# Global-query scores as eight 64x32 products over two key halves, with maxima exchanged on GpSimd

## The chip, the cores and the metric

The kernel runs on one core of one Trainium2 chip. A core has a matrix engine (TensorE; PE in the rows, with PEld for its weight loads), a vector engine (VectorE, DVE), a scalar engine (ScalarE, ACT), GpSimd (POOL), a queue engine (SyncE, SP) and 16 DMA engines. SBUF is the working memory of 128 partitions, PSUM the memory of 8 banks into which TensorE writes. The metric is the device time of one execution in microseconds (us); lower is better.

## What is computed

Two stages, all in float32. First attention, with batch 8, 8 heads, 512 local and 32 global tokens of width 64. Each global query looks at all 544 keys; each local query looks at the 32 global keys and at the local keys within 32 positions. Then a soft mixture of experts over the 4352 resulting rows.

```
k_all = np.concatenate([k_g, k_l], axis=2)
s_g   = scale * np.matmul(q_g, k_all.transpose(0, 1, 3, 2))
out_g = np.matmul(sm(s_g), v_all)                  # sm: exp(s - max) / (sum + 1e-9)
s_l   = scale * [q_l @ k_g.T, where(|i - j| <= 32, q_l @ k_l.T, -1e9)]
out_l = np.matmul(sm(s_l), np.concatenate([v_g, v_l], axis=2))
x     = rows of concatenate([out_g, out_l], axis=2)
logits = x @ phi                                   # then softmax over tokens and over slots,
slot_out[e] = relu(slot_input[e] @ w1[e]) @ w2[e]  # experts, and c @ slot_out
```

The change concerns `s_g` and `sm(s_g)` alone.

## The kernel before

Attention runs in 32 steps. Step s handles two heads: the upper 64 partitions of the tile `kq` hold the transposed keys and queries of one head, the lower 64 those of the other. Every engine runs its instructions in the order in which the program issues them; `step(s)` writes that order by hand. In step s TensorE does, in this order: scores of step s+1 into the PSUM tile `pS` (`scores`; it begins with the mask products that read `cb`), turns of the shifted scores of step s into `pT` (`turn_pair`, operands `con,w`), turns of finished rows (`con,x`) and of shifted global scores (`con,sgs`) into `pM`, value products of step s-1 into `pO` (`values`, first with 32 columns, last with 64), and between those, in odd steps, the value products of global queries (`v,eg`) and the logits (`xT,phisb`, when s % 4 = 1) or the token sums (`x,dd`, when s % 4 = 3).

Global queries are handled for two steps, that is four heads, at once: i = s // 2 runs from 0 to 15. Four heads of 32 queries fill 128 partitions.

- `global_scores(i)` (line 309) stands last on TensorE in the even step 2i. The query operand has 64 columns, 32 for each of two heads, and zeros in the other head's partitions, so that a product over all 128 partitions gives both heads. Per `kq` tile there is a product of 480 key columns into bank 0 of `pM` and one of 64 into bank 1. ScalarE copies both into `sgr` (608 columns).
- `global_max(i)` (line 321) reduces `sgr` on VectorE to `gm` in the odd step; `global_shift(i)` (line 325) subtracts the maximum on ScalarE, `sgr` to `sgs`, near the end of the odd step, behind `og`.
- `turn_global` turns `sgs` on TensorE in the next two steps, `exp_global` takes the exponential on ScalarE into `eg`, and `global_values` multiplies by the values.

At the end of an odd step VectorE normalises the step's rows (`x`, line 303) and computes `rg` (line 365) for the global queries before; ScalarE scales them (`og`, line 371), shifts (`sgs`, line 326) and, when s % 4 = 1, copies the logits out of `pM` (`lT`, line 544). When s % 4 = 3 VectorE adds the token sums (`acc`, line 449). The next step's turns on TensorE write the banks that `lT` and `acc` read, and read `sgs`.

GpSimd makes two shifted copies of the values per step (`make_v`, `va` and `vb`) and, in odd steps, four copies of `og` into `xg`.

Loads of `kq`, `v` and of expert weights `w` are issued by `pump` whenever the count `npe` of TensorE instructions passes a multiple of 256 after `PHASE`; the load then waits for that TensorE instruction. A float32 product counts as four instructions: two passes, each with a weight load. After the steps come the experts, which the change leaves as they were.

Of the kernel before, what the change touches and what calls it, by code (L numbers as in the profile page):

```python
# [17 lines left out]
P = 128  # L18
VD = D + 1
NP = 4 * B  # L20
NEG = -8.0e9
GUARD = 1e-9
SCALE = 0.125

ROW0, ROW1, QONE, ROW2, GCOPY, SQ = 0, 6, 11, 12, 17, 23
SQG = SQ + 15
NSLOT = SQG + 2  # L30
KQC = 32 * NSLOT


BANKS = [[0, 13, 11, 12], [1, 4, 7, 10], [2, 5, 8, 14], [3, 6, 9, 15]]
PAIRED = ((0, 0), (2, 3))
IN_ROW = [(q, i) for i in range(4) for q in range(4) if (q, i) != (3, 1)]
Q_SLOT = {(3, 1): QONE, **{qi: SQ + k for k, qi in enumerate(IN_ROW)}}
BLK_POS = {c: (k, i) for k, cs in enumerate(BANKS) for i, c in enumerate(cs)}
TOK = {4: 0, 7: 1}
LW = P + NS  # L40
GW = 608
VG = (0, 1, 2, 3, 5)

C_ID, C_Q, C_EM, C_ONE = 0, 128, 256, 258
# [22 lines left out]
def kernel(ctx, tc, kq, vS, phi, w1, w2, cst, cbf, out):  # L67
    nc = tc.nc
# [16 lines left out]
    pM = psum.tile([P, 2, 512], F32, name="pM")  # L85
# [13 lines left out]
    dT = keep.tile([P, LW], F32, name="dT")  # L99
    dd = keep.tile([P, P], F32, name="dd")  # L100
    de = keep.tile([P, NS], F32, name="de")
    sgr = at.tile([P, GW], F32, name="sgr")
    sgs = at.tile([P, GW], F32, name="sgs")
    eg = at.tile([P, 5, P], F32, name="eg")

    def bc(ap, n):
# [17 lines left out]
    def mm(o, l, r, start=True, stop=True):  # L124
        return counted(2 if l.dtype == BF16 else 4, nc.tensor.matmul(o, l, r, start=start, stop=stop))  # L125
# [180 lines left out]


    def global_scores(i):
        for pp in range(2):
            k = kqs[2 * i + pp]  # L310
            q = k[:, SQG:SQG + 2, :]
            mm(pM0[HALF[pp], 0:480], q, at_cols(k, FULL, 0, [(192, 3), (32, 5), (1, 32)]))
            mm(pM1[HALF[pp], 0:64], q, at_cols(k, FULL, 32 * 5, [(32 * (GCOPY - 5), 2), (1, 32)]))
        nc.scalar.copy(at_cols(sgr, FULL, 0, [(32, 3), (P, 5), (1, 32)]),
                       pM0[:, 0:480].rearrange("p (r m j) -> p r m j", r=3, m=5))
        nc.scalar.copy(at_cols(sgr, FULL, 480, [(-384, 2), (1, 32)]),
                       pM1[:, 0:64].rearrange("p (a j) -> p a j", a=2))

    gm = {}

    def global_max(i):
        gm[i] = xp.tile([P, 1], F32, tag="gm", name=f"gm{i}")
        nc.vector.tensor_reduce(gm[i], sgr, axis=AX.X, op=ALU.max, negate=True)

    def global_shift(i):
        nc.scalar.activation(sgs, sgr, AF.Identity, bias=gm[i])  # L326


    def turned(c, n, w=P, t=pM):
        return t[0:w, :, c:c + 64 * n].rearrange("p r (u q) -> p u r q", q=64)  # L330

# [10 lines left out]

    def turn_global(n, c0=CG, t=pM):
        units = []
        for u, m in enumerate((0, 1, 2) if n == 0 else (3, 5)):
            lo, w = (P * m, 96 if m == 3 else P) if m < 4 else (480, P)
            units.append(turn_to(c0 + 64 * u, sgs[:, lo:lo + w], w, t))
        return both(units)

    def exp_global(n, c0=CG, t=pM):  # L350
        for m, u, k, w in (((0, 0, 3, P),) if n == 0 else ((3, 0, 1, 96), (4, 1, 1, P))):
            nc.scalar.activation(split(eg[0:w, m:m + k, :]), turned(c0 + 64 * u, k, w, t), AF.Exp, scale=SCALE)  # L352

    def global_values(i, bank):
        for n, m in enumerate(VG):
            for j in range(4):
                mm(bank[32 * j:32 * j + 32, 0:VD], eg[:, n, 32 * j:32 * j + 32],
                   vs[2 * i + j // 2][:, m, j % 2, :], n == 0, n == 4)

    rgs = {}  # L360
# [99 lines left out]
    for _ in range(4):  # L460
        issue(queue)
    nc.sync.dma_start(phisb, phi)
    nc.gpsimd.memset(sgr, NEG)
    nc.gpsimd.memset(eg, 0.0)
    nc.vector.memset(guard, GUARD)
    nc.scalar.activation(lrun, guard, AF.Exp)
    npe[0] = 48
# [5 lines left out]
    def step(s):  # L473
# [64 lines left out]
        if q == 2 and s >= 6:  # L538
            totals(b - 1)
        if not ev:  # L540
            global_shift(i)
        if q == 1 and b >= 1:
            w = LW if b - 1 in TOK else P
# [17 lines left out]
    exp_global(0)  # L561
    nc.scalar.copy(split(dd.unsqueeze(1)), turned(CD, 1))
    copy_tokens(s - 2, nc.vector.tensor_copy)
    global_shift(i)
    values(s - 1, (1,))
    global_values(i - 1, gO)
# [284 lines left out]
def _layout(inputs):  # L851
# [8 lines left out]

    rows = [list(range(0, 16, 3)), list(range(1, 16, 3)), list(range(2, 16, 3))]
    both = np.concatenate([chunks(k_l, k_g), chunks(q_l, q_g)], axis=2)
    seq = rows[0] + rows[1] + [17 + BANKS[3][1]] + rows[2] + [16] * 6 + [17 + BANKS[q][i] for q, i in IN_ROW] + [33, 33]
    kq = both[:, :, seq].reshape(B, 4, 2, KQC, D).transpose(0, 1, 2, 4, 3).reshape(NP, P, NSLOT, 32)
    kq = np.ascontiguousarray(kq)
    kq[:, 64:, SQG] = 0
    kq[:, :64, SQG + 1] = 0
    vc = np.ones((B, H, 17, 32, VD), q_l.dtype)
    vc[..., :D] = chunks(v_l, v_g)
    vseq = sum([[3 * m, 3 * m + 1, 3 * m + 2, 16] for m in range(5)], []) + [15, 12, 13, 14]  # L870
# [48 lines left out]
```

## Time and profile before

| | us |
|---|---|
| timed runs | 264.94, 266.04, 268.48 (median 266.04) |
| the profiled execution | 264.19 |
| its span, first to last instruction | 262.4 |
| TensorE busy | 228.8 (87%) |
| VectorE busy | 161.2 (61%) |
| ScalarE busy | 118.7 (45%) |
| GpSimd busy | 100.9 (38%) |

Busy time is an average over the attention steps (about 10 to 195 us) and the experts behind them. The chain of waits follows the work that ended last back from the end; "issue" in it is time in which an engine waited for nothing that the profile shows. A matmul's time in a row includes the time in the array's pipeline, so that consecutive products overlap in the rows; how long a stage holds TensorE is read from the start of its first row to the start of the next stage.

### The profile page before, as it was taken

The numbers are of one execution on the slowest core, as the hardware profiler recorded it, in microseconds if no ns is written. First come the engines' busy times: TensorE is split into PE (matmuls) and PEld (weight loads), VectorE is DVE, ScalarE is ACT, GpSimd is POOL, SyncE is SP. The second block draws the span as 40 slices with busy tenths as digits, with TensorE's granted clock in tenths as the row PEclk, the third lists the DMA queues.
The fourth block names the chain that finished last, engine by engine and source line by source line (L and its number), as shares of the span: only waits on it lengthen the run. The fifth ranks groups of instructions, "written<-read, shape, count | busy, mean of one in ns | idle before, by whom it ended". The sixth has DMA issues, their size and how long they took to land.

```text
span 262.4 us, 14172 instructions
## 1 busy us (share of the span) xinstructions
PE 228.8 (87%) x6435; PEld 157.8 (60%) x6435; DVE 161.2 (61%) x281; ACT 118.7 (45%) x292; POOL 100.9 (38%) x196
## 2 busy tenths in 40 slices
PE   8789988998998998899799988969879999999910
PEld 5477666686766757576675865757655344545700
DVE  0777756876777775767577868745634673144810
ACT  2235727556555653656545555715832031132810
POOL 2484537384482835547380845534510000000000
PEclk9999999999999999999999999997999999999975
DMA  7958968779879687776868687798999999985997
GB/s 237 374 206 254 331 237 257 249 289 299 288 252 318 210 275 229 276 257 235 333 188 313 217 302 273 241 374 336 303 382 361 417 406 410 408 317 198 370 352 256
DMA packets 26636, 77.61 MB, mean 296 GB/s; under 512 B 2384, under 2 KB 8784, under 8 KB 26576
## 3 DMA queue, kind: packets, MB, share of 16 engines
q1 hardware_dynamic: 22400, 65.12, 70.7%
q10 hardware_dynamic: 4176, 11.58, 12.1%
q8 instruction: 50, 0.82, 1.2%
q14 instruction: 10, 0.08, 0.1%
HBM read 67.78 MB, written 8.91 MB: 292 GB/s over the span
## 4 chain that ended last, share of the span: by engine, by line
PE 73%; DVE 10%; issue 7%; ACT 5%; ACTq 0%; DVEq 0%
PE pO L125 16%; PE pS L125 12%; PE pM L125 11%; PE pM L128 6%; PE kT L125 5%; PE kM L125 5%; PE pT L128 4%; PE kS L125 4%; PE kO L125 4%; DVE x L303 3%; PE pM L456 2%; DVE mx L249 2%; DVE w L251 1%; ACT sgs L326 1%; DVE acc L449 1%
## 5 line engine op out<-in xcount | busy, mean ns | idle before, releaser
L249 DVE TENSOR_REDUCE mx<-pS 128x8 f32<-128x1024 f32 x31 | 37.7, 1217 | 16.5 <-PE pS L125 16.5
L125 PE MATMUL pS<-kq 64*64 64x128 f32 (+1 forms) x1736 | 41.2, 279 | 3.8 <-issue 3.8
L375 POOL COPY xg<-og 32x64 f32<-32x64 f32 x62 | 14.3, 231 | 75.1 <-ACT og L371 73.2
L125 PE MATMUL pO<-v,w 128*32 128x65 f32 x620 | 40.6, 224 | 1.0 <-issue 0.9
L125 PE MATMUL pO<-va,w 128*32 128x65 f32 x620 | 40.9, 226 | 0.0
L251 DVE TENSOR_TENSOR w<-pS,mx 128x1024 f32<-128x1024 f32 x31 | 38.0, 1225 | 1.1
L125 PEld LDWEIGHTS pS<-kq 64*64 64x64 f32 (+1 forms) x1736 | 30.8, 111 | 12.6 <-issue 10.2
L125 PEld LDWEIGHTS pO<-v,w 128*32 128x32 f32 x620 | 32.1, 115 | 8.2 <-issue 6.5
L258 ACT ACTIVATE w<-pT 128x1024 f32<-128x1024 f32 x32 | 32.5, 1017 | 9.2 <-PE pT L128 9.2
L125 PEld LDWEIGHTS pO<-va,w 128*32 128x32 f32 x620 | 31.9, 115 | 3.0 <-issue 1.0
L352 ACT ACTIVATE eg<-pM 96x128 f32<-96x128 f32 (+2 forms) x45 | 13.9, 343 | 33.3 <-PE pM L128 32.6
L267 POOL COPY va<-v 128x650 f32<-128x650 f32 x32 | 23.2, 725 | 13.0 <-DMA v<-in_vS_dram 11.7
L125 PE MATMUL pO<-vb,w 128*32 128x65 f32 x496 | 27.6, 221 | 0.4 <-issue 0.4
L292 ACT ACTIVATE r<-pO,guard 128x8 f32<-128x8 f32 x31 | 8.3, 267 | 39.1 <-PE pO L125 39.0
L128 PE MATMUL pT<-con,w 64*128 64x64 f32 x512 | 23.1, 230 | 1.6 <-DVE w L251 0.8
L268 POOL COPY va<-v 32x650 f32<-32x650 f32 x32 | 23.1, 722 | 2.0
L128 PEld LDWEIGHTS pT<-con,w 64*128 64x128 f32 x512 | 18.6, 139 | 8.2 <-issue 2.9
L303 DVE TENSOR_TENSOR x<-pO,r 128x512 f32<-128x512 f32 x31 | 21.4, 692 | 3.2
L125 PEld LDWEIGHTS pO<-vb,w 128*32 128x32 f32 x496 | 22.2, 109 | 0.6 <-issue 0.6
L295 DVE RECIPROCAL r<-r 128x8 f32<-128x8 f32 x32 | 6.5, 202 | 23.5 <-ACT r L292 23.3
L269 POOL COPY vb<-v 64x520 f32<-64x520 f32 x32 | 19.8, 620 | 1.9
L270 POOL COPY vb<-v 64x520 f32<-64x520 f32 x32 | 19.7, 614 | 1.7
(204 smaller groups left out, 429.7 us busy)
## 6 DMA issues: line engine op xcount, KB each, us to landing
w<-in_w_dram SPq DMA_DIRECT2D x60, 512.0 KB, 6.3
kq<-in_kq_dram SPq DMA_DIRECT2D x32, 640.0 KB, 4.9
v<-in_vS_dram ACTq DMA_DIRECT2D x29, 390.0 KB, 5.1
out_dram<-ob SPq DMA_DIRECT2D x16, 512.0 KB, 4.6
xw<-in_w_dram SPq DMA_DIRECT2D x4, 512.0 KB, 7.0
v<-in_vS_dram SPq DMA_DIRECT2D x3, 390.0 KB, 6.9
out_dram<-ob SPq DMA_DIRECT2D x2, 256.0 KB, 4.8
cb<-in_cbf_dram SPq DMA_DIRECT2D x1, 272.0 KB, 2.9
```

The lines of the kernel that those rows point to most:

```text
L125: return counted(2 if l.dtype == BF16 else 4, nc.tensor.matmul(o, l, r, start=start, stop=stop))
L128: return counted(2, nc.tensor.transpose(o, src, idn))
L249: nc.vector.reduce_max(mx, g, axis=AX.X)
L251: nc.vector.tensor_tensor(ws[s], g, bc(mx, P), ALU.subtract)
L258: nc.scalar.activation(ws[s], pT.rearrange("p r (u q) -> p (r u q)", q=64), AF.Exp, scale=SCALE)
L267: nc.gpsimd.tensor_copy(va, v[:, 0:5])
L268: nc.gpsimd.tensor_copy(va[0:32], v[0:32, 1:6])
L269: nc.gpsimd.tensor_copy(vb[64:128], v[64:128, 0:4])
L270: nc.gpsimd.tensor_copy(vb[0:64], v[0:64, 1:5])
L303: nc.vector.tensor_tensor(xs[b][:, :, P * p:P * p + P].rearrange("p t (h d) -> p h t d", h=2), o[:, :, :, 0:D], bc(r.rearrange("p (h t) -> ...
L352: nc.scalar.activation(split(eg[0:w, m:m + k, :]), turned(c0 + 64 * u, k, w, t), AF.Exp, scale=SCALE)
L375: copy(xgs[b // 4][32 * (b % 4):32 * (b % 4) + 32, D * hd:D * hd + D], og[32 * j:32 * j + 32, :])
```

## The change

The query operand has 32 columns and no zeros. Each head's product runs over its own 64 partitions, and the 576 key columns (the 17 chunks of 32 keys, with the global chunk twice) are taken in two halves of 288: half x goes into bank x of `pM`. For a `kq` tile pp, a partition half hh and a key half x the output goes to partitions 32c to 32c+31 with c = 2pp + (hh xor x): in the second half neighbouring heads have changed places. So eight products of 64 partitions, 32 output partitions and 288 columns stand in place of four, on eight different parts of the array. One ScalarE copy of 576 columns brings them to `sgr`.

Each half has its own maximum (`gx`, two columns), and since the halves of a head lie on different partitions, GpSimd copies `gx` to `gy` with neighbouring groups of 32 partitions exchanged (four copies of 32x2); `global_both` on VectorE combines the two into `gm`, one column for each half. The shift becomes three ScalarE instructions of 288, 192 and 64 columns with a bias from `gm`; `sgs`, now 640 columns wide, is filled once with NEG where `eg` was cleared before. The second exponential becomes one instruction where there were two, and all turns have 128 columns. The value products of the second half read `eg` with the heads changed back. The size of `kq` stays the same: a second zero-padded query slot is given up, and `QONE` moves into the row of queries.

```
-ROW0, ROW1, QONE, ROW2, GCOPY, SQ = 0, 6, 11, 12, 17, 23
-SQG = SQ + 15
-NSLOT = SQG + 2
+ROW0, ROW1, GONE, ROW2, GCOPY, SQ = 0, 6, 11, 12, 17, 23
+SQG = SQ + 16
+NSLOT = SQG + 1
...
     def global_scores(i):
-        for pp in range(2):
-            k = kqs[2 * i + pp]
-            q = k[:, SQG:SQG + 2, :]
-            mm(pM0[HALF[pp], 0:480], q, at_cols(k, FULL, 0, [(192, 3), (32, 5), (1, 32)]))
-            mm(pM1[HALF[pp], 0:64], q, at_cols(k, FULL, 32 * 5, [(32 * (GCOPY - 5), 2), (1, 32)]))
-        nc.scalar.copy(at_cols(sgr, FULL, 0, [(32, 3), (P, 5), (1, 32)]),
-                       pM0[:, 0:480].rearrange("p (r m j) -> p r m j", r=3, m=5))
-        nc.scalar.copy(at_cols(sgr, FULL, 480, [(-384, 2), (1, 32)]),
-                       pM1[:, 0:64].rearrange("p (a j) -> p a j", a=2))
+        for x in range(2):
+            for hh in range(2):
+                for pp in range(2):
+                    k, c = kqs[2 * i + pp], 2 * pp + (hh ^ x)
+                    mm(pM[32 * c:32 * c + 32, x, 0:GH], k[HALF[hh], SQG, :],
+                       at_cols(k, HALF[hh], 96 * x, [(192, 3), (32, 3), (1, 32)]))
+        nc.scalar.copy(sgr, pM[:, :, 0:GH])
...
     def global_max(i):
-        gm[i] = xp.tile([P, 1], F32, tag="gm", name=f"gm{i}")
-        nc.vector.tensor_reduce(gm[i], sgr, axis=AX.X, op=ALU.max, negate=True)
+        gx[i] = [xp.tile([P, 2], F32, tag=n, name=f"{n}{i}") for n in ("gx", "gy")]
+        nc.vector.tensor_reduce(gx[i][0], sgr, axis=AX.X, op=ALU.max, negate=True)
+        for c in range(4):
+            R, O = (slice(32 * k, 32 * k + 32) for k in (c, c ^ 1))
+            nc.gpsimd.tensor_copy(gx[i][1][R], gx[i][0][O])
+
+    def global_both(i):
+        gm[i] = xp.tile([P, 2], F32, tag="gm", name=f"gm{i}")
+        x, y = gx.pop(i)
+        nc.vector.tensor_tensor(gm[i], x, at_cols(y, FULL, 1, [(-1, 2)]), ALU.min)
...
     def global_shift(i):
-        nc.scalar.activation(sgs, sgr, AF.Identity, bias=gm[i])
+        for c, d, dst, src in ((0, 0, [(32, 3), (P, 3), (1, 32)], [(96, 3), (32, 3), (1, 32)]),
+                               (3 * P, GH, [(32, 3), (160, 2), (1, 32)], [(96, 3), (32, 2), (1, 32)]),
+                               (4 * P, GH + 64, [(-32, 2), (1, 32)], [(192, 2), (1, 32)])):
+            nc.scalar.activation(at_cols(sgs, FULL, c, dst),
+                                 bass.AP(sgr.tensor, sgr.offset + d, [list(sgr.ap[0])] + [list(e) for e in src]),
+                                 AF.Identity, bias=gm[i][:, (c > 0):(c > 0) + 1])
...
     def exp_global(n, c0=CG, t=pM):
-        for m, u, k, w in (((0, 0, 3, P),) if n == 0 else ((3, 0, 1, 96), (4, 1, 1, P))):
-            nc.scalar.activation(split(eg[0:w, m:m + k, :]), turned(c0 + 64 * u, k, w, t), AF.Exp, scale=SCALE)
+        k = 3 - n
+        nc.scalar.activation(split(eg[:, 3 * n:3 * n + k, :]), turned(c0, k, P, t), AF.Exp, scale=SCALE)
...
         if not ev:
+            global_both(i)
             global_shift(i)
```

On TensorE, at the end of an even step, the order before (a row of a product stands for its two passes; `kq_294` and `kq_387` are the tiles of the two steps):

```order
L125 MATMUL pO<-v_296,w_381 64x65
L125 MATMUL pO<-va_458,w_381 64x65
L125 MATMUL pM<-kq_294 64x480
L125 MATMUL pM<-kq_294 64x64
L125 MATMUL pM<-kq_387 64x480
L125 MATMUL pM<-kq_387 64x64
L125 LDWEIGHTS cb
```

and now (the same place; `kq_282` and `kq_388` are the same two tiles):

```order
L126 MATMUL pO<-v_284,w_396 64x65
L126 MATMUL pO<-va_471,w_396 64x65
L126 MATMUL pO<-v_284,w_396 64x65
L126 MATMUL pO<-va_471,w_396 64x65
L126 MATMUL pM<-kq_282 32x288
L126 MATMUL pM<-kq_388 32x288
```

The last two rows come four times in turn, and then the mask products (`cb`) follow as before: eight products with 32 output partitions where four with 64 stood.

On ScalarE, at the end of an odd step with s % 4 = 1 and the start of the next, before:

```order
L258 ACTIVATE w_646<-pT 128x1024
L371 ACTIVATE og_881<-pO,rg_878 128x64
L326 ACTIVATE sgs<-sgr,gm_765 128x608
L544 COPY lT<-pM 128x128
L352 ACTIVATE eg<-pM 96x128
L352 ACTIVATE eg<-pM 128x128
L385 COPY xT_965<-pM 128x512
```

and now:

```order
L259 ACTIVATE w_668<-pT 128x1024
L385 ACTIVATE og_910<-pO,rg_907 128x64
L338 ACTIVATE sgs<-sgr,gm_916 128x3x3x32
L338 ACTIVATE sgs<-sgr,gm_916 128x3x2x32
L338 ACTIVATE sgs<-sgr,gm_916 128x2x32
L558 COPY lT<-pM 128x128
L365 ACTIVATE eg<-pM 128x256
L399 COPY xT_997<-pM 128x512
```

Three shifts stand between `og` and `lT` where one stood; behind the turns one exponential stands for two.

On VectorE, from the reduction of `sgr` in an odd step with s % 4 = 3 to the next step, now (before, the fourth last row was not there, and the first wrote `gm`, one column):

```order
L324 TENSOR_REDUCE gx_1089<-sgr 128x2
L296 RECIPROCAL r_1192<-r_1192 128x8
L304 TENSOR_TENSOR x_905<-pO,r_1192 128x2x4x64
L378 TENSOR_SCALAR rg_1197<-pO 128x1
L379 RECIPROCAL rg_1197<-rg_1197 128x1
L332 TENSOR_TENSOR gm_1206<-gx_1089,gy_1090 128x2
L461 COPY acc<-pM 128x512
L250 TENSOR_REDUCE mx_1250<-pS 128x8
L252 TENSOR_TENSOR w_1252<-pS,mx_1250 128x1024
```

The combining step stands behind four other instructions after the reduction; between the two, GpSimd has its four copies `gy`, ahead of `xg`.

## Rows read from the trace of the kernel before

**Rows 1.** The page: busy us and instructions, a queue (packets, MB), the chain.
```profile
PE 228.8 (87%) x6435; PEld 157.8 (60%) x6435; DVE 161.2 (61%) x281; ACT 118.7 (45%) x292; POOL 100.9 (38%) x196
...
q8 instruction: 50, 0.82, 1.2%
...
PE 73%; DVE 10%; issue 7%; ACT 5%; ACTq 0%; DVEq 0%
```

**Rows 2.** Attention: busy PE, PEld, DVE, ACT, POOL (instructions); clock, DMA share, GB/s.
```profile
10.00:195.00 185.00, 165.27 (x5652) 124.24 (x5652) 130.37 (x204) 99.83 (x244) 99.02 (x190) 0.99 0.81 276
```

**Rows 3.** Waits of TensorE, 10 to 195 us: total us, times, longest.
```profile
PE pS L125 <- issue: 5.5, 4, 1.7
...
PE pM L125 <- issue: 3.6, 3, 2.4
...
PE pO L125 <- issue: 2.6, 5, 0.9
...
PE pS L125 <- DVE w L251: 1.3, 2, 0.7
```

**Rows 4.** TensorE by time, end of an even step: start, us, what.
```profile
97.55 0.22 PE L125 MATMUL pO<-va,w 128*64 128x65 f32 x1
...
98.67 0.41 PE L125 MATMUL pS<-cb 64*64 64x512 bf16 x4
```

**Rows 5.** TensorE by time, end of an odd step.
```profile
93.26 0.22 PE L125 MATMUL pO<-va,w 128*64 128x65 f32 x1
93.41 0.41 PE L125 MATMUL pS<-cb 64*64 64x512 bf16 x4
```

**Rows 6.** TensorE by time, four 32x32 products into one bank, experts' start.
```profile
200.03 0.63 PE L125 MATMUL kM<-xg,de 32*32 32x256 f32 x8
200.60 0.42 PE L125 MATMUL kM<-x,dd 128*32 128x256 f32 x4
```

**Rows 7.** ScalarE by time, end of an odd step with logits.
```profile
83.79 0.31 ACT L371 ACTIVATE og<-pO,rg 128x64 f32<-128x64 f32 x1 [0.48 <-DVE rg L365]
84.00 0.79 ACT L326 ACTIVATE sgs<-sgr,gm 128x608 f32<-128x608 f32 x1
84.70 0.25 ACT L544 COPY lT<-pM 128x128 f32<-128x128 f32 x1
```

**Rows 8.** TensorE by time behind it.
```profile
85.00 0.46 PE L128 MATMUL pM<-con,x 64*128 64x64 f32 x8 [0.85 <-ACT lT L544]
```

**Rows 9.** ScalarE and TensorE by time, ends of two odd steps with token sums.
```profile
51.33 0.79 ACT L326 ACTIVATE sgs<-sgr,gm 128x608 f32<-128x608 f32 x1
...
52.18 0.32 PE L128 MATMUL pM<-con,sgs 64*96 64x64 f32 x4
...
166.34 0.79 ACT L326 ACTIVATE sgs<-sgr,gm 128x608 f32<-128x608 f32 x1
...
167.19 0.32 PE L128 MATMUL pM<-con,sgs 64*96 64x64 f32 x4
```

**Rows 10.** GpSimd by time in an odd step; a two-operand VectorE instruction, min/median/max ns.
```profile
84.17 1.05 POOL L375 COPY xg<-og 32x64 f32<-32x64 f32 x4 [4.43 <-ACT og L371]
...
L415 DVE TENSOR_TENSOR nm<-bm,nm x7: 159/160/1124, 65.2 to 197.7; 128x1 f32<-128x1 f32 x7
```

**Rows 11.** The last step by time: GpSimd, ScalarE, TensorE.
```profile
186.48 0.62 POOL L270 COPY vb<-v 64x520 f32<-64x520 f32 x1
...
187.22 0.80 ACT L326 ACTIVATE sgs<-sgr,gm 128x608 f32<-128x608 f32 x1 [0.57 <-DVE gm L323]
...
192.03 0.77 PE L125 MATMUL pS<-v,eg 128*32 128x65 f32 x39 [1.72 <-issue]
```

**Rows 12.** The chain in time: its longest pause.
```profile
174.17 2.37 issue
```

**Rows 13.** The stretch behind that pause, columns as in rows 2.
```profile
177.50:181.00 3.50, 3.50 (x77) 2.44 (x78) 1.32 (x5) 2.24 (x5) 0.60 (x3) 0.51 0.89 343
```

More of the change, by code (lines that the diff above doesn't have):

```diff
@@ L35 @@
 PAIRED = ((0, 0), (2, 3))
-IN_ROW = [(q, i) for i in range(4) for q in range(4) if (q, i) != (3, 1)]
-Q_SLOT = {(3, 1): QONE, **{qi: SQ + k for k, qi in enumerate(IN_ROW)}}
+IN_ROW = [(q, i) for i in range(4) for q in range(4)]
+Q_SLOT = {qi: SQ + k for k, qi in enumerate(IN_ROW)}
 BLK_POS = {c: (k, i) for k, cs in enumerate(BANKS) for i, c in enumerate(cs)}
@@ L40 @@
 LW = P + NS
-GW = 608
+GH = 288
 VG = (0, 1, 2, 3, 5)
@@ L101 @@
     de = keep.tile([P, NS], F32, name="de")
-    sgr = at.tile([P, GW], F32, name="sgr")
-    sgs = at.tile([P, GW], F32, name="sgs")
+    sgr = at.tile([P, 2, GH], F32, name="sgr")
+    sgs = at.tile([P, 5 * P], F32, name="sgs")
     eg = at.tile([P, 5, P], F32, name="eg")
@@ L319 @@
-    gm = {}
-    def global_max(i):
-        gm[i] = xp.tile([P, 1], F32, tag="gm", name=f"gm{i}")
-        nc.vector.tensor_reduce(gm[i], sgr, axis=AX.X, op=ALU.max, negate=True)
-    def global_shift(i):
-        nc.scalar.activation(sgs, sgr, AF.Identity, bias=gm[i])
+        for x in range(2):
[4 more added lines that the diff above has]
+                       at_cols(k, HALF[hh], 96 * x, [(192, 3), (32, 3), (1, 32)]))
@@ new lines, in global_scores @@
+        nc.scalar.copy(sgr, pM[:, :, 0:GH])
+    gm, gx = {}, {}
+    def global_max(i):
+        gx[i] = [xp.tile([P, 2], F32, tag=n, name=f"{n}{i}") for n in ("gx", "gy")]
[7 more added lines that the diff above has]
+        nc.vector.tensor_tensor(gm[i], x, at_cols(y, FULL, 1, [(-1, 2)]), ALU.min)
@@ L344, in turn_global @@
         units = []
-        for u, m in enumerate((0, 1, 2) if n == 0 else (3, 5)):
-            lo, w = (P * m, 96 if m == 3 else P) if m < 4 else (480, P)
-            units.append(turn_to(c0 + 64 * u, sgs[:, lo:lo + w], w, t))
+        for u, m in enumerate((0, 1, 2) if n == 0 else (3, 4)):
+            units.append(turn_to(c0 + 64 * u, sgs[:, P * m:P * m + P], P, t))
         return both(units)
     def exp_global(n, c0=CG, t=pM):
-        for m, u, k, w in (((0, 0, 3, P),) if n == 0 else ((3, 0, 1, 96), (4, 1, 1, P))):
-            nc.scalar.activation(split(eg[0:w, m:m + k, :]), turned(c0 + 64 * u, k, w, t), AF.Exp, scale=SCALE)
+        k = 3 - n
+        nc.scalar.activation(split(eg[:, 3 * n:3 * n + k, :]), turned(c0, k, P, t), AF.Exp, scale=SCALE)
     def global_values(i, bank):
@@ L356, in global_values @@
             for j in range(4):
-                mm(bank[32 * j:32 * j + 32, 0:VD], eg[:, n, 32 * j:32 * j + 32],
+                c = j if n < 3 else j ^ 1
+                mm(bank[32 * j:32 * j + 32, 0:VD], eg[:, n, 32 * c:32 * c + 32],
                    vs[2 * i + j // 2][:, m, j % 2, :], n == 0, n == 4)
@@ L462 @@
     nc.sync.dma_start(phisb, phi)
-    nc.gpsimd.memset(sgr, NEG)
-    nc.gpsimd.memset(eg, 0.0)
+    nc.gpsimd.memset(sgs, NEG)
     nc.vector.memset(guard, GUARD)
@@ L563 @@
     copy_tokens(s - 2, nc.vector.tensor_copy)
+    global_both(i)
     global_shift(i)
@@ L862, in _layout @@
     both = np.concatenate([chunks(k_l, k_g), chunks(q_l, q_g)], axis=2)
-    seq = rows[0] + rows[1] + [17 + BANKS[3][1]] + rows[2] + [16] * 6 + [17 + BANKS[q][i] for q, i in IN_ROW] + [33, 33]
+    seq = rows[0] + rows[1] + [16] + rows[2] + [16] * 6 + [17 + BANKS[q][i] for q, i in IN_ROW] + [33]
     kq = both[:, :, seq].reshape(B, 4, 2, KQC, D).transpose(0, 1, 2, 4, 3).reshape(NP, P, NSLOT, 32)
     kq = np.ascontiguousarray(kq)
-    kq[:, 64:, SQG] = 0
-    kq[:, :64, SQG + 1] = 0
     vc = np.ones((B, H, 17, 32, VD), q_l.dtype)
```

## The prediction, made before the result was known

> **What bounds the kernel now.** I read the shares of the chain first, to see which engine ends last: TensorE holds 73% of it and VectorE 10% [rows 1]. So the reader should look for time that leaves or enters TensorE's stream. Attention is next, from 10 to 195 us: TensorE is busy there for 165.27 of 185 us [rows 2]. Then the waits of TensorE in that stretch: the largest is "issue", 5.5 + 3.6 + 2.6 = 11.7 us in twelve pauses [rows 3], in which nothing that the profile shows held it. What is it? The page has 50 packets, 0.82 MB in all, on the instruction queue, 16 KB each, and TensorE and its loads have 2 x 6435 = 12870 instructions [rows 1], some 257 for a packet. Counted through the trace, these pauses lie 256 instructions or a multiple of it apart. I conclude that TensorE waits for its own instructions: its stream is limited by work and by fetching at once. A block of 256 lasts 185 x 256 / (5652 + 5652) = 4.19 us [rows 2].
>
> The other limit is the end of the odd steps. With s % 4 = 1 ScalarE runs `og`, `sgs`, `lT`, and TensorE's next turn waits 0.85 us for `lT` [rows 7, 8]. With s % 4 = 3 `sgs` ends at 51.33 + 0.79 = 52.12, and the turns that read it begin at 52.18; at the last of these steps 167.13 and 167.19 [rows 9]. Going through all odd steps, I find three of the first kind in which `lT` holds TensorE and seven of the second in which `sgs` does; in the others fetching or other work is later.
>
> **The change part by part.**
>
> *The products.* Now the last row of the value products starts at 97.55 and the mask products at 98.67: the stage holds TensorE for 1.12 us [rows 4]. After it, three parts. Entering another tile shape costs 0.15 us, as from values to mask products in an odd step (93.26 to 93.41) [rows 5]. Four 32x32 products of 256 columns, two passes each, hold the array for 200.60 - 200.03 = 0.57 us [rows 6]. With 288 columns this is 0.03 us more per pass, and four more products starting a few ns apart add some 0.03: 0.66. Together 0.81 us, a saving of 0.31 per pair of steps. It counts in 14 of 16: after the first, scores wait for VectorE anyway (1.3 us in two waits) [rows 3], and after the last no scores follow. **-4.3 us.** Its bounds are 0.54 less (below, if products take turns, a loss) and 0.15 more, if the change of shape costs nothing.
>
> Do eight products run side by side? The four of [rows 6] have four row groups and write into one bank at the same time, on different partitions; the new ones differ only in using both banks. [...]
>
> *ScalarE's shift.* From `og` (64 columns) to `sgs` it is 0.21 us, from `sgs` (608) to `lT` 0.70 [rows 7]: 0.49 / 544 = 0.90 ns a column and 0.15 us per instruction. Three with 544 columns take 0.46 + 0.49 = 0.95, which is 0.25 more. This lies between `og` and what TensorE waits for, in ten odd steps: **+2.5 us.** Bounds: 1.0 if it shows in four only, 3.8 in fifteen. The saved copy of `sgr` and the joined exponential stand where TensorE has other work (values), so I cost them at nothing; if that cover were gone they would be a gain of some 0.1 us a step pair.
>
> *The exchange of maxima.* Four GpSimd copies of 32x64 take 1.05 us [rows 10]; those of 32x2 take no more. GpSimd sat idle for 4.43 us before them [rows 10], waiting for `og`, and behind the new copies stand only `xg` and the next `make_v`, which wait for later events than the reduction. `global_both` stands four instructions behind the reduction on VectorE, after `rg`, and costs like the two-operand row: 160 ns when GpSimd is idle, up to 1124 when its copies run at the same time [rows 10]; here it is idle. `gm` is ready before `og` ends, so `sgs` does not wait; what stands behind it on VectorE is `acc`, 0.16 later, but ahead of `sgs`. Nothing, with 1 us as the upper bound over all steps.
>
> In the last step it is different. GpSimd is in `make_v` until 186.48 + 0.62 = 187.10, and `sgs` starts at 187.22 [rows 11]. With up to 1.05 us of copies, the combination and 0.25 more shift, the turns come up to 1.4 us later, and `exps` with them, which is queued behind on ScalarE. But a fetch pause of 1.72 us ends at 192.03 [rows 11], behind the same turns, and covers it if it stays. **+0.3 us** (0 to 1.4).
>
> *Instructions.* Eight products are 32 instructions where 16 were, 256 more in 16 pairs: one more block to fetch. Where TensorE waits for fetching, faster products give nothing, and a block more costs its full turn. Bounds: nothing, if fetching is always ahead, and 4.2, a block's time. With twelve pauses spread over all of attention I take nearer the upper end: **+3.0 us.** Loads are paced by the same count, so they move with it; their number is the same.
>
> *Turns of 128 columns for 96* differ by a few ns: nothing.
>
> Sum: 264.19 - 4.3 + 2.5 + 0.3 + 3.0 = 265.7, that is 1.5 more than the profiled execution. This one was faster than all three timed runs (median 266.04), so I put the difference on the median: **267.5 us**.
>
> **The rivals.**
>
> *Fetching costs nothing.* Then -4.3 + 2.5 + 0.3 gives -1.5: 264.5 us. For it: most blocks show no pause. Against: twelve do, and the saving makes blocks shorter. [...]
>
> *The products take turns* (the other side). If the two partition halves share a bank only in turn, the stage needs two more passes of 0.27: 0.81 + 0.54 = 1.35, longer than 1.12 now. 14 x 0.54 = 7.6 us more: 275.1. It decides as soon as four of the eight start a pass late. Against it: [rows 6].
>
> [...]
>
> *The shift is covered.* If other waits hide it, as fetching does in some steps, and fetching is also free, -4.3 + 0.3 gives 262.0.
>
> **How the numbers follow.** Forecast 0.62, its own range 265 to 270; fetching free 0.18; turns 0.07; one or two more long pauses 0.08; shift covered 0.05. Leaving out turns, the case of two more pauses and the last case gives 263.2 to 271.5: free fetching less 1.3 for a shift covered in half the steps, and one more pause with 0.9 for a dearer last step. Within 2% (5.3 us), which is about what a measurement of this kernel can tell from no change, lie forecast, free fetching and covered shift but for small tails, and half of the pauses: 0.83. Slower: turns 0.07, two pauses 0.04, a tail of 0.02, together 0.13. Faster than 260.7 would need all losses gone and a stage under 0.7 us: 0.04.
>
> **What would show it.** From the last value row of an even step to the mask products 0.81 us, with eight products starting within some 60 ns; 1.35 would show turns. From the first shift to `lT` 0.95, and TensorE waiting for `lT` or `sgs` by 0.25 more. `gm` done before `og` ends, in all but the first and last step; if VectorE waits for `gy`, the exchange was mispriced. 51 packets on the instruction queue, and more than 11.7 us of "issue" between 10 and 195 us; if this sum falls, the forecast is wrong at that step.

## The result, and the profile after

The changed kernel takes 269.1 us (median; 268.15 to 275.16), the kernel before 266.4 us in the runs taken beside it. The ratio is 1.0116 [1.0085, 1.0147] (in brackets its 95% interval): 3.1 us slower, by the interval 2.3 to 3.9, and thus within 2%. The forecast was 267.5 us, 1.5 above the median, in a range from 263.2 to 271.5. The forecast's case came in, with a sum that was 1.6 us too low. Ratios leave disturbed executions out; in f3_248_idle_apart and b3_again below these were more than half, the profiled one of the former among them, which is why one has a wide interval and the other no ratio.

The profiled execution took 268.76 us, 0.3 under the median of its kernel; that of the kernel before took 264.19, 2.2 under its median. The two profiles are thus further apart than the kernels, and a difference of 2 us in one row of them carries little. The page of the kernel after: the busy engines, the clock over 40 slices, the instruction queue, the chain by engine and by line.

```profile
span 266.9 us, 14524 instructions
...
PE 224.3 (84%) x6563; PEld 153.2 (57%) x6563; DVE 162.7 (61%) x297; ACT 121.8 (46%) x292; POOL 111.2 (42%) x259
...
PEclk9999999999999999999999999999999999999985
...
q8 instruction: 51, 0.84, 1.2%
...
PE 69%; issue 9%; DVE 9%; ACT 7%; POOL 1%; ACTq 0%; DVEq 0%; POOLq 0%
PE pO L126 16%; PE pS L126 12%; PE pM L126 8%; PE kT L126 5%; PE kM L126 5%; PE pM L129 5%; PE pT L129 4%; PE kS L126 4%; ACT sgs L338 4%; PE kO L126 3%; DVE x L304 2%; DVE w L252 2%; PE pM L470 2%; DVE mx L250 2%; ACT r L293 1%
```

Against [rows 1], TensorE is busy for 4.5 us less, and yet the span is 4.5 us longer. TensorE's share of the chain fell from 73% to 69%; "issue" rose from 7% to 9% and ScalarE from 5% to 7%, of which the shift alone (`ACT sgs L338`) has 4%. So the time went into waiting. Which waits? The waits of TensorE from 10 to 200 us (total us, times, longest):

```profile
PE pM L129 <- ACT lT L558: 4.7, 5, 1.2
PE pS L126 <- issue: 4.3, 7, 0.9
PE pM L126 <- issue: 4.2, 3, 2.3
...
PE pO L126 <- issue: 3.5, 4, 1.2
...
PE pM L129 <- ACT sgs L338: 2.0, 7, 0.6
PE pM L129 <- issue: 2.0, 2, 1.1
...
PE pS L129 <- ACT sgs L338: 1.3, 2, 1.1
```

In the kernel before, from 10 to 195 us, [rows 3] and these:

```profile
PE pM L128 <- ACT lT L544: 2.5, 3, 0.8
...
PE pM L128 <- issue: 0.5, 1, 0.5
PE pT L128 <- issue: 0.4, 1, 0.4
PE pM L128 <- ACT sgs L326: 0.4, 1, 0.4
PE pS L128 <- ACT sgs L326: 0.3, 1, 0.3
```

"Issue" in these rows is 14.0 us, with a short wait of `pT` 14.4, where it was 12.6: the 11.7 us in twelve pauses of the prediction left out the two short rows here, so that its sign, more than 11.7 us, was set 0.9 too low. A wait for ScalarE now leads, `lT`, and together with `sgs` it is 8.0 us, where it was 3.2. Counted through TensorE's instructions, the 17 pauses of "issue" of the kernel after between 10 and 200 us lie a multiple of 256 apart, to within one, as the 14 before do.

To see the whole of attention I summed all TensorE records from 10 us to the first turn of the experts (`kT<-xT`), from the start of each to the start of the next, and took the waits of 150 ns and more out by what ended them. What is left is called work. All kernels below are counted in this way, each from its one profiled execution:

| kernel | whole | work | issue | `lT` and `sgs` | other waits |
|---|---|---|---|---|---|
| before | 184.7 | 165.1 | 12.6 | 3.2 | 3.7 |
| after | 188.9 | 161.2 | 14.5 | 8.0 | 5.0 |
| after, a second time | 188.4 | 161.4 | 12.9 | 7.9 | 6.0 |
| after with one shift (a1) | 187.1 | 161.5 | 15.8 | 3.8 | 5.8 |
| after without exchange (a2) | 190.1 | 162.1 | 16.4 | 6.6 | 4.8 |
| products alone (a4) | 187.0 | 162.8 | 15.8 | 2.7 | 5.5 |
| after, shift first (a3) | 189.0 | 164.2 | 17.7 | 3.1 | 3.8 |
| before with three shifts (b1) | 187.7 | 167.3 | 12.7 | 4.5 | 3.0 |
| before, shift first (b3) | 183.5 | 165.5 | 13.9 | 1.0 | 2.9 |

Two things other than work are in that column. A wait counts from the modelled end of the matmul ahead of it, and a shorter one than 150 ns does not count; what is left of it stays in work. And the clock: in every profile of the table but the two of the kernel after, attention has a stretch of 3.4 us at half clock, which takes 1.7 us; a4 has two. (The mean granted clock of the profiled execution is 0.983 in both profiles of the kernel after, 0.968 in a4, 0.975 before, and 0.973 to 0.978 in the others.)

The change took 3.9 us of work out of attention, 1.7 of them the clock, and put 8.1 us of waits in: 4.8 for ScalarE's `lT` and `sgs`, 1.9 for instructions, 1.3 for other things (the exponential `w`, the copy `dd`, the sums `acc`). On equal clock work fell by 2.2 us, though the stages of the products shrank by more (4.6, below); what longer and more frequent waits leave in the column is the likely reason, but this is not shown. The waits for `lT` and `sgs` are the steady part, since both profiles of the kernel after show them alike; "issue" is not, with 14.5 and 12.9.

TensorE by time, at the end of an even step, answers [rows 4]:

```profile
102.14 0.22 PE L126 MATMUL pO<-v,w 128*64 128x65 f32 x1
102.14 0.22 PE L126 MATMUL pO<-va,w 128*64 128x65 f32 x1
102.29 0.72 PE L126 MATMUL pM<-kq 64*32 64x288 f32 x16
102.94 0.41 PE L126 MATMUL pS<-cb 64*64 64x512 bf16 x4
```

From the last value row to the mask products it is 0.80 us, where it was 1.12. The row with x16 holds the eight products with two passes each; in the single records the first passes all start between 102.290 and 102.337, the second ones between 102.557 and 102.603. Eight products thus run side by side.

ScalarE and then TensorE by time, at the end of an odd step with logits, answer [rows 7] and [rows 8]; the step is the one with the longest such wait:

```profile
183.73 0.31 ACT L385 ACTIVATE og<-pO,rg 128x64 f32<-128x64 f32 x1 [0.47 <-DVE gm L332]
183.95 1.11 ACT L338 ACTIVATE sgs<-sgr,gm 128x288 f32<-128x288 f32 x3
184.96 0.25 ACT L558 COPY lT<-pM 128x128 f32<-128x128 f32 x1
```

```profile
185.26 0.47 PE L129 MATMUL pM<-con,x 64*128 64x64 f32 x8 [1.16 <-ACT lT L558]
185.56 0.29 PE L129 MATMUL pM<-con,sgs 64*128 64x64 f32 x4
```

From the first shift to `lT` it is 1.01 us, where it was 0.70. TensorE waits 1.16 us for `lT`, where it was 0.85. (The row of `og` names `gm` as what ended the wait, where it was `rg`; but in the trace `og` starts 0.09 us after the end of `rg` in both kernels, so the combining step does not delay it.)

### The profile page after: what moved, and what is told of

It reads as the page before. It is cut to its first block, busy times and chain, and to the rows that moved or that the text cites. A ratio compares the mean times of both kernels' runs of the same rounds, so it can differ in the third digit from the quotient of the medians.

```text
span 266.9 us, 14524 instructions
## 1 busy us (share of the span) xinstructions
PE 224.3 (84%) x6563; PEld 153.2 (57%) x6563; DVE 162.7 (61%) x297; ACT 121.8 (46%) x292; POOL 111.2 (42%) x259
## 3 DMA queue, kind: packets, MB, share of 16 engines
q10 hardware_dynamic: 4176, 11.58, 11.7%
## 4 chain that ended last, share of the span: by engine, by line
PE 69%; issue 9%; DVE 9%; ACT 7%; POOL 1%; ACTq 0%; DVEq 0%; POOLq 0%
PE pO L126 16%; PE pS L126 12%; PE pM L126 8%; PE kT L126 5%; PE kM L126 5%; PE pM L129 5%; PE pT L129 4%; PE kS L126 4%; ACT sgs L338 4%; PE kO L126 3%; DVE x L304 2%; DVE w L252 2%; PE pM L470 2%; DVE mx L250 2%; ACT r L293 1%
## 5 line engine op out<-in xcount | busy, mean ns | idle before, releaser
L126 PEld LDWEIGHTS pS<-kq 64*64 64x64 f32 (+1 forms) x1736 | 30.2, 109 | 13.3 <-issue 10.4
L365 ACT ACTIVATE eg<-pM 128x256 f32<-128x256 f32 (+1 forms) x30 | 13.1, 438 | 30.5 <-PE pM L129 29.2
L327 POOL COPY gy<-gx 32x2 f32<-32x2 f32 x64 | 11.4, 178 | 29.2 <-DVE gx L324 26.2
L270 POOL COPY vb<-v 64x520 f32<-64x520 f32 x32 | 19.8, 619 | 1.8
```

Source lines behind the costliest of these rows:

```text
L270: nc.gpsimd.tensor_copy(vb[64:128], v[64:128, 0:4])
L327: nc.gpsimd.tensor_copy(gx[i][1][R], gx[i][0][O])
L365: nc.scalar.activation(split(eg[:, 3 * n:3 * n + k, :]), turned(c0, k, P, t), AF.Exp, scale=SCALE)
```

## The experiments

**One shift in the kernel after.** The three instructions become one of 544 columns with one bias.

```
-        for c, d, dst, src in ((0, 0, ...), (3 * P, GH, ...), (4 * P, GH + 64, ...)):
-            nc.scalar.activation(at_cols(sgs, FULL, c, dst), ..., bias=gm[i][:, (c > 0):(c > 0) + 1])
+        nc.scalar.activation(sgs[:, 0:544], bass.AP(sgr.tensor, sgr.offset, [list(sgr.ap[0]), [1, 544]]),
+                             AF.Identity, bias=gm[i][:, 0:1])
```

> The changed kernel with the shift of the global scores as one ScalarE instruction of 544 columns with one bias instead of three with two (the shifted scores then stand in other columns, and two of the four heads are shifted by another head's maximum). Theory A, the three-part shift lengthens the way from og to TensorE's next turn: first shift to lT falls from 1.01 us (trace of the changed kernel) to about 0.64, and the time falls by 2 to 4 us against the changed kernel, to about 265 to 267. Rival, the time went to fetching instructions alone: no change, 268 to 269, since fetching then takes up what the shift frees.

Measured: 267.04 us, ratio to the kernel before 1.0022 [0.9979, 1.0066]. Against the 1.0116 of the kernel after, the three parts cost 0.0094, about 2.5 us (roughly 1 to 4 by the two intervals). In the table the waits for `lT` and `sgs` fall by 4.2 us, but "issue" is 1.3 higher than in the one profile of the kernel after and 2.9 higher than in the other: part of what one wait gives back, another takes.

**Three shifts in the kernel before.** The same cut from the other side, with nothing else changed.

```
-        nc.scalar.activation(sgs, sgr, AF.Identity, bias=gm[i])
+        for lo, hi in ((0, 288), (288, 480), (480, 608)):
+            nc.scalar.activation(sgs[:, lo:hi], sgr[:, lo:hi], AF.Identity, bias=gm[i])
```

> The kernel before with its shift cut in three ScalarE instructions of 288, 192 and 128 columns, the same values. Theory A: first shift to lT rises from 0.70 to about 1.05 us, and the time by 2.5 to 4 us over the kernel before (ratio 1.010 to 1.015). Rival, the shift is hidden behind fetch pauses: under 1 us.

Measured: 268.48 us, ratio 1.0122 [1.007, 1.0173], that is 3.2 us (1.9 to 4.6). Cutting the shift in three costs the kernel before as much as the whole change costs it. Here the profile's waits of TensorE are (from 10 to 200 us, columns as above)

```profile
PE pS L125 <- issue: 6.0, 4, 1.8
PE pM L128 <- ACT lT L545: 4.1, 4, 1.2
PE pM L125 <- issue: 3.6, 3, 2.6
PE pO L125 <- issue: 3.0, 6, 1.1
...
PE pM L128 <- ACT sgs L327: 0.5, 1, 0.5
```

The wait for `lT` is 4.1 us where the kernel before has 2.5, and "issue" stays, 12.7 against 12.6 in the table. There the waits for `lT` and `sgs` grow by 1.3 us only, and work by 2.2, though TensorE runs the same matmuls in the same order as in the kernel before. Taken from start to start, matmul by matmul, attention is 3.4 us longer, and some 3 of these lie between the last turn of `w` and the last turn of `sgs`, where TensorE waits for ScalarE. So the loss to ScalarE's shift is shown from both sides: 2.5 us taken away, 3.2 us added.

**No exchange.** The four GpSimd copies are left out, and each half uses its own row's other maximum.

```
-        for c in range(4):
-            R, O = (slice(32 * k, 32 * k + 32) for k in (c, c ^ 1))
-            nc.gpsimd.tensor_copy(gx[i][1][R], gx[i][0][O])
...
-        nc.vector.tensor_tensor(gm[i], x, at_cols(y, FULL, 1, [(-1, 2)]), ALU.min)
+        nc.vector.tensor_tensor(gm[i], x, at_cols(x, FULL, 1, [(-1, 2)]), ALU.min)
```

> The changed kernel without GpSimd's four copies; each half is shifted by its own partitions' two maxima, so part of the heads get another head's maximum. The prediction costs the exchange at nothing but for the last step (0 to 1.4 us): 0 to 1 us less than the changed kernel. Rival, GpSimd's copies or VectorE's wait for them hold the odd steps: 2 us less or more.

Measured: 268.55 us, ratio 1.0137 [1.0082, 1.0193], not below that of the kernel after. No gain by taking the exchange away can be seen. In its profile TensorE's waits for `sgs` are some 1.2 us shorter than in the kernel after, most of that in the last step (0.39 for 1.13), too little to show in the time. Why the exchange is hidden in the steps between, GpSimd and then VectorE of the kernel after show, by time in an odd step:

```profile
142.76 0.83 POOL L327 COPY gy<-gx 32x2 f32<-32x2 f32 x4 [2.13 <-DVE gx L324]
146.63 1.04 POOL L389 COPY xg<-og 32x64 f32<-32x64 f32 x4 [3.03 <-ACT og L385]
```

```profile
141.89 0.74 DVE L324 TENSOR_REDUCE gx<-sgr 128x2 f32<-128x576 f32 x1
144.90 0.20 DVE L296 RECIPROCAL r<-r 128x8 f32<-128x8 f32 x1 [2.26 <-ACT r L293]
145.21 0.69 DVE L304 TENSOR_TENSOR x<-pO,r 128x512 f32<-128x512 f32 x1
145.81 0.15 DVE L378 TENSOR_SCALAR rg<-pO 128x1 f32<-128x1 f32 x1
146.00 0.16 DVE L379 RECIPROCAL rg<-rg 128x1 f32<-128x1 f32 x1
146.08 0.14 DVE L332 TENSOR_TENSOR gm<-gx,gy 128x2 f32<-128x2 f32 x1
```

The copies end at 143.59, and the combining step takes its place at 146.08 without a wait. Over the kernel, 0.4 us is all that VectorE waited for `gy`, once, in the last step.

**The products alone.** The kernel after with one shift and no exchange: what is left is the eight products, the joined copy and exponential, and 256 more instructions. Its edit is that of the two kernels above, together.

> The kernel after with both other parts of the change taken away: one shift of 544 columns with one bias in place of three, and no copies on GpSimd (so maxima of the two halves are not exchanged and the output is not the reference's). What is left of the change is the eight products, the joined copy and exponential, and 256 more TensorE instructions. By the prediction's terms -4.3 + 3.0 gives 1.3 us less than the kernel before, ratio 0.995 (0.988 to 1.000); if fetching were free it would be 0.984. If the exchange costs nothing, it equals the kernel after with one shift, which was at 1.0022.

Measured: 267.10 us, ratio 1.0034 [0.9993, 1.0075]. The products alone gain nothing, although work is 2.3 us lower in its profile, and 4.0 on equal clock (it has two stretches of 3.4 us at half clock and a mean of 0.968, where the kernel before has one and 0.975). "Issue" is 3.2 us higher and the other waits 1.8: in these two profiles the array's saving went into waits that stood behind it.

**256 more instructions in the kernel before, by cutting products.** Each product of 480 columns becomes one of 320 and one of 160, each of 64 becomes two of 32.

```
-            mm(pM0[HALF[pp], 0:480], q, at_cols(k, FULL, 0, [(192, 3), (32, 5), (1, 32)]))
-            mm(pM1[HALF[pp], 0:64], q, at_cols(k, FULL, 32 * 5, [(32 * (GCOPY - 5), 2), (1, 32)]))
+            mm(pM0[HALF[pp], 0:320], q, at_cols(k, FULL, 0, [(192, 2), (32, 5), (1, 32)]))
+            mm(pM0[HALF[pp], 320:480], q, at_cols(k, FULL, 384, [(32, 5), (1, 32)]))
+            mm(pM1[HALF[pp], 0:32], q, at_cols(k, FULL, 32 * 5, [(1, 32)]))
+            mm(pM1[HALF[pp], 32:64], q, at_cols(k, FULL, 32 * GCOPY, [(1, 32)]))
```

> The kernel before with its four global products cut in eight by columns (480 as 320 and 160, 64 as 32 and 32), the same work and 256 more TensorE instructions in all, as many as the change adds. If a block of instructions more costs a fetch turn: 2 to 4 us over the kernel before, with 51 packets on the instruction queue and more issue time on TensorE. If fetching is hidden: under 0.5 us, the stage from the last value row to the mask products staying near 1.12 us.

Measured: 276.64 us, ratio 1.0421 [1.0364, 1.0478], far more than either theory said. The experiment doesn't isolate fetching: the stage from the last value row to the mask products went from 1.12 to 2.05 us, though the columns are the same, and 0.93 in 14 pairs of steps is 13 us. The single records show where the time went. In the kernel before the passes of 480 columns start in pairs in all sixteen stages, the first passes 5 to 14 ns apart and the second ones 13 to 56: the products of the two `kq` tiles run side by side. Here the four passes of 320 columns start one after another, 0.30, 0.84 and 1.16 us behind the first in the stage at 104.23: the second tile comes after the first. Why the cut undoes the overlap is not shown. "Issue" in attention fell from 12.6 to 10.9 us, with 51 packets. What follows is only that a block more did not show here while TensorE was held by its own work.

**256 empty instructions in the kernel before.** To add instructions without products, 16 no-operations stand behind the score products.

```
             mm(pM1[HALF[pp], 0:64], q, at_cols(k, FULL, 32 * 5, [(32 * (GCOPY - 5), 2), (1, 32)]))
+        for _ in range(16):
+            nc.tensor.nop(hint="x", nofuse=True)
+            npe[0] += 1
```

> The kernel before, with 16 empty instructions (no-operations, nothing for the array to do) behind the four score products of each pair of steps: 256 more on TensorE in all, the number that the change adds. The instruction queue then has 51 packets where the kernel before has 50. If a block more to fetch costs TensorE its turn, as the prediction's +3.0 us says, the time is 1.5 to 4 us above the kernel before (ratio 1.006 to 1.015) and 'issue' between 10 and 195 us rises from 11.7 to 13 or more. If fetching has reserve, or the gap that 16 empty instructions open in the stream is filled by work already queued, the ratio is 0.997 to 1.003 and the sum of 'issue' stays within 1 us. If empty instructions themselves cost the sequencer time that the array sees, the stage from the last value row to the mask products becomes longer than 1.12 us, and that length times 15 is to be taken off first.

Measured: 269.51 us, ratio 1.0156 [1.0073, 1.0239], 4.2 us more, with 51 packets. "Issue" is 15.1 us in attention, 2.5 more, in a profile of the slowest of its six executions (271.36 us). The stage is 1.18 us where nothing else lies in it and mostly up to 1.25 in others, so 0.06 to 0.13 in 14 pairs, some 1 to 2 us, is the empty instructions' own. This leaves some 2 to 3 us for the block, inside a wide interval.

**512 empty instructions**, 32 in the same place.

> The kernel before with 32 empty instructions (no-operations) behind the four score products of each pair of steps, twice those of the kernel with 16: 512 more on TensorE, 52 packets on the instruction queue. With 256 the ratio was 1.0156 [1.0073, 1.0239], about 4.2 us. If each block of 256 costs TensorE its turn in attention, 512 cost twice that: 6 to 10 us, ratio 1.023 to 1.038, and 'issue' grows by some 5 us over that of the kernel before. If the 4.2 us were what the empty instructions themselves take (0.06 us of 1.12 in the stage, about 1 us in all, is all that the rows show) the stage from the last value row to the mask products grows by as much as the time. If the 4.2 us came from where the pauses happened to fall, the ratio stays near 1.01 to 1.02.

Measured: 281.66 us, ratio 1.0594 [1.0539, 1.0649]. It fails as a dose, for the stage grew to between 2.35 and 2.68 us; here it is 2.42, TensorE by time:

```profile
105.86 0.22 PE L125 MATMUL pO<-va,w 128*64 128x65 f32 x1
105.91 1.14 PE L125 MATMUL pM<-kq 128*64 128x480 f32 x8
108.28 0.41 PE L125 MATMUL pS<-cb 64*64 64x512 bf16 x4 [1.23 <-DVE x L303]
```

The products are over 1.14 us after 105.91, and the mask products begin 1.23 later. (The row names VectorE's `x` as what ended the wait, but the same stage has no such wait with 16 empty instructions: it is they that take the time, by estimate 2.37 us / 32 = 0.074 us each.) Some 1.3 us in 14 pairs are 18 us, more than the 15.8 that the kernel lost; "issue" is 13.3. As with the cut products ("issue" 10.9), the added blocks did not show here while the stream was slow for another reason.

**248 empty instructions, in two places.** Eight behind the score products, whose 1.08 us cover them, and eight in odd steps behind the logits or token sums.

```
+        for _ in range(8):
+            nc.tensor.nop(hint="x", nofuse=True)
+            npe[0] += 1
...
             sums(b - 1, pM1)
+        if not ev:
+            for _ in range(8):
+                nc.tensor.nop(hint="x", nofuse=True)
+                npe[0] += 1
```

> The kernel before with its empty instructions in two places: 8 behind the four score products of each pair of steps, and 8 behind the logits or token sums of each odd step before the last, 248 in all, 51 packets. With 16 in one place the stage from the last value row to the mask products rose from 1.12 to between 1.18 and 1.25 us, and with 32 to 2.45: 16 more took 1.25 us, so one takes about 0.08 us of the sequencer, and 8 take 0.64, which the 1.08 us of products ahead of them cover. So here the stage should be 1.12 again, and the empty instructions take nothing of their own. If the block more to fetch costs its turn, the ratio is 1.007 to 1.015 and 'issue' rises by 2 to 4 us; if the 4.2 us of the kernel with 16 were the empty instructions' own time, it is 0.998 to 1.005.

Measured: ratio 1.0032 [0.9967, 1.0097], with 51 packets. The stage is 1.12 again in most steps, so the empty instructions are covered, as meant. But the interval reaches from a gain of 0.9 us to a loss of 2.6 and holds both theories' lower ends; and its profile is not used for "issue". This run settles nothing; it speaks for a block's price below 3 us.

**The shift first.** In the kernel after, the combining step moves up behind the step's reciprocal, and the shifts ahead of `og`, into time in which ScalarE waits.

```
             recip(s - 1)
+            if not ev:
+                global_both(i)
             normalise(s - 1)
+        if not ev:
+            global_shift(i)
         if not ev and i >= 1:
             global_recip(i - 1, gO)
             global_out(i - 1, gO)
...
-        if not ev:
-            global_both(i)
-            global_shift(i)
```

> The kernel after with an order changed and nothing else: the combining step on VectorE moves up behind the reciprocal of the step, and the three shifts on ScalarE move ahead of og, into the 0.47 us in which ScalarE waits for rg. In the kernel after the shifts could begin at 87.83 instead of 88.51, so sgs would end some 0.65 us earlier and lT some 0.36 earlier, and og 0.65 later. If ScalarE's shift is what keeps TensorE waiting (4.7 us for lT in 5 waits and 3.3 for sgs in 9 by the kernel after's rows), 3 to 6 us come back: 263 to 266 us, ratio 0.988 to 1.000. If TensorE's fetching takes its place, the waits for lT and sgs fall but 'issue' grows, and the ratio stays at 1.005 to 1.012. If og, now later, is what holds the next work (GpSimd's xg, va and vb behind it), TensorE shows new waits for va or vb.

Measured: 268.19 us, ratio 1.0074 [1.0022, 1.0126]. The order does what it should: the turns of finished rows now follow the step's other turns at once, as TensorE by time shows, 0.54 us after the first of those and with no wait,

```profile
85.81 0.71 PE L129 MATMUL pT<-con,w 64*128 64x64 f32 x16
86.35 0.41 PE L129 MATMUL pM<-con,x 64*128 64x64 f32 x8
```

and the waits for `lT` and `sgs` fall from 8.0 to 3.1 us. But "issue" rises to 17.7, and only about 1 us of the time comes back, or 2 against the second measurement of the kernel after (the intervals overlap, so even that is not certain). Its waits of TensorE, from 10 to 200 us:

```profile
PE pO L126 <- issue: 6.5, 8, 1.3
PE pS L126 <- issue: 4.8, 7, 2.2
PE pM L126 <- issue: 3.9, 4, 2.2
PE pS L126 <- DVE w L252: 2.0, 2, 1.3
PE pM L129 <- ACT lT L559: 1.7, 3, 0.6
```

This is the second of the three theories: take the wait for ScalarE away, and the wait for instructions takes its place.

**The shift first, in the kernel before.** The same move with its one shift.

> The kernel before with the same change of order: its one shift ahead of og on ScalarE; gm is ready long before. Its waits of TensorE for lT and sgs between 10 and 195 us are 2.5 and 0.7 us, so at most 3 us can come back: 263 to 266, ratio 0.989 to 1.000. The theory that the three shifts are the loss of the change says that this order gains less here than in the kernel after; if it gains as much, the order is worth that by itself and says nothing about the change.

> The kernel before with its one shift ahead of og, a second time: the first gave 0.9971 [0.9926, 1.0016]. If the order is a gain of its own, the ratio is again 0.993 to 0.999 and the waits of TensorE for lT stay at 1 us where the kernel before has 2.5; if it was a chance of the runs, it lies at 0.999 to 1.005.

Measured: 264.83 us, ratio 0.9971 [0.9926, 1.0016]; the second time, no ratio came out (262.69 to 268.70 us in six executions, against 264.04 to 267.74). The waits for `lT` and `sgs` went from 3.2 to 1.0 and 1.2 us in the two profiles, "issue" from 12.6 to 13.9 and 14.8. A kernel that is faster than both has not been shown.

**The kernel after once more.**

> The kernel after, unchanged, on the chip and in the call of the run beside it. If nothing but the change made its time, the ratio is again 1.0116 within 0.004, and TensorE's waits between 10 and 200 us are those of its first profile within 1 us each: about 4.7 for lT, 3.3 for sgs, 14.5 of issue. The four kernels with the eight products had 14.5 to 17.7 of issue so far, so this part may well vary by 2 us.

Measured: 269.94 us, ratio 1.0155 [1.0098, 1.0212]. The time repeats. The waits for `lT` and `sgs` are 7.9 us, within 0.1 of the first profile; "issue" is 12.9, 1.6 less. A single profile's "issue" is thus good to about 2 us, which is as much as the block in question.

## Why the prediction came out, term by term

**The products (-4.3): right.** The stage is 0.80 us against a forecast of 0.81, with starts within 47 ns; over all pairs of steps the sixteen stages add up to 4.6 us less, all of it in the fourteen that were counted on (3.6 in the second profile, where pauses fell into some of them). The rival that they take turns by bank (1.35) is refuted for this case: products of both partition halves that write into the same bank did so at once here, all eight in 0.72 us.

**The shift (+2.5): right in place and size.** First shift to `lT` took 0.31 us more, where 0.25 was forecast. By itself it costs 2.5 us (taken away) or 3.2 (added). The waits for `lT` and `sgs` in the profile grow by more, 4.8 us, since in the first and in the last odd step the exchange stands in the way too: 0.65 in the first, where there was no such wait, and 1.0 more in the last (below). The other 3.2 us are of the size that the two experiments give. All in all these waits now bind in 14 places, where it was 5 before.

**The exchange (0, in the last step 0.3): right between, and in the last step by the luck of a pause.** In all but the first and last odd step `gm` stands ready, as forecast. In the last step the chain is long, as VectorE, GpSimd, ScalarE and TensorE show in turn:

```profile
190.12 0.74 DVE L324 TENSOR_REDUCE gx<-sgr 128x2 f32<-128x576 f32 x1
...
191.86 0.16 DVE L332 TENSOR_TENSOR gm<-gx,gy 128x2 f32<-128x2 f32 x1 [0.40 <-POOL gy L327]
```

```profile
190.99 0.84 POOL L327 COPY gy<-gx 32x2 f32<-32x2 f32 x4
```

```profile
192.12 1.12 ACT L338 ACTIVATE sgs<-sgr,gm 128x288 f32<-128x288 f32 x3 [1.63 <-DVE gm L332]
```

```profile
192.70 0.40 PE L129 MATMUL pS<-con,sgs 64*128 64x64 f32 x6 [1.13 <-ACT sgs L338]
...
196.06 0.65 PE L126 MATMUL pS<-v,eg 128*32 128x65 f32 x31 [0.68 <-issue]
```

`sgs` begins 1.26 us after the reduction's end, where it was 0.09 [rows 11] (the reduction then ended at 187.13), and TensorE waits 1.13 for it, where it was 0.3. But the fetch pause behind the turns shrank from 1.72 [rows 11] to 0.68, so that 1.04 came back: in this profile the cover held, as the prediction put it. In the second profile of the same kernel the wait is 1.13 again, but the pause is 1.50, so that 0.22 came back. The 0.3 is thus right in one profile of two; the bounds of the term, 0 to 1.4, hold both.

**The block of instructions (+3.0): the step that rests on least.** The 51 packets came, and "issue" in the waits is above 11.7 us in both profiles of the kernel after (14.0 and 12.9). But against the tally's 12.6 before it rose by 1.9 and 0.3 only; in the kernels that carry the products, a1, a2 and a4, by 3.2 to 3.8, and in a3 by 5.1. Empty instructions gave 4.2 us with some 1 to 2 of their own, and 0.9 in the other arrangement. So a price between nothing and 3 us fits, and 3.0 is at its upper end. What the runs bear out better is the sentence ahead of it: where TensorE waits for fetching, faster products give nothing. With three shifts and exchange gone, the products still bring no gain (1.0034), where a free fetch would have given 0.984; that it is fetching which takes the saving, and not the other waits, is argued from single profiles. The rival of free fetching does not agree with that: pauses still come block after block, as at 29.29, 33.39 and 37.49 us in the kernel after (0.93, 0.46 and 1.20 us long), each 256 instructions behind the last, to within one.

**What the sum lacked.** Products and block together were put at -1.3; a4, which has both and little else, is at +0.9 (from -0.2 to +2.0 by its interval). This is the term that was mis-sized, and it is larger than the miss of the whole, 1.6 us. The prediction priced a block's turn, but not that TensorE, arriving sooner, waits more for other things too: the other waits in the tally are 1.3 to 2.3 us above those before in the two profiles of the kernel after, and 1.8 in a4 (the copy `dd`, the exponential `w`, the guard step `r`). How much of the 2.2 us is this and how much is fetching stays open.

**The clock.** The case of one or two more long pauses (0.08) did not come in; in the profiles it went the other way. In the kernel before the granted clock was 0.51 for 3.5 us behind a pause of 2.37 us [rows 12, 13], by estimate a loss of up to 3.5 x 0.49 = 1.7 us. In the kernel after, the chain has a pause as long, and the clock stays whole behind it; the chain by time, and then the stretch behind it (columns as in [rows 2]):

```profile
178.47 2.34 issue
```

```profile
180.50:185.00 4.50, 3.30 (x103) 2.44 (x102) 2.45 (x7) 2.45 (x7) 0.77 (x4) 1.00 0.78 305
```

By that estimate it is 1.7 us in favour of the kernel after, in this one execution, and on equal clock the two profiles would be as much further apart. Its second profile has a pause of 2.62 us and a whole clock behind it too (its mean granted clock is 0.983, as in the first); the profiles of all other kernels here have one or two stretches near 0.5 in attention, at different places (means of 0.967 to 0.978). The upper end of the forecast's range counts one more long pause at 3.1 us (271.5 - 0.9 - 267.5). No run shows that term; the pauses of 2.34 and 2.62 us had no loss of clock behind them. The times do not rest on this: over the executions that the ratios use, the mean granted clock is 0.974 and 0.975 for the kernel after and 0.970 to 0.973 for the kernel before.

## What to carry to other kernels

Where the waits of an engine are "issue", a stage that is made shorter is not a saving yet: read what is next behind it, and count the instructions that the shorter form needs. Here 4.5 us off the array, with 256 more instructions, came to no gain even without the rest of the change. A short instruction that was cut in three on an engine whose end another engine waits for took 0.31 us more here at each such place (1.01 for 0.70), while work put into an engine's idle time with a consumer that came 2.5 us later (the exchange, but for the first and last step) cost nothing that could be measured (1.0137 without it, 1.0116 with it).

## What was not expected of the hardware

- An empty instruction was not free on TensorE: 32 of them lengthened a stage from 1.12 to 2.42 us, by estimate 0.074 us each, and 16 hid behind 1.08 us of products but for 0.06 to 0.13.
- Cutting products into several with fewer columns on the same part of the array was dear: with the same columns in eight products in place of four the stage took 2.05 us for 1.12 (b2), since the two halves of the array no longer worked side by side, while eight products on eight parts took 0.80.
- After a pause of 2.34 us the granted clock stayed at 1.00, and in the second profile (mean 0.983, as in the first) after one of 2.62, where after one of 2.37 it had been 0.51: a pause's length alone did not decide it.
